# Which queue carries the divisions and the sum rows in a fused decay-attention and MLP kernel

## The chip, the cores and the metric

The kernel runs on one core of a Trainium2 chip. Its metric is the time of one execution in device microseconds, lower is better; a version's figure is the median of its runs. The profile is of one execution, whose own time is given beside its span. The engines are TensorE (PE, with its weight loads listed apart), VectorE (DVE), ScalarE (ACT), GpSimd (POOL) and SyncE (SP). SP computes nothing and issues transfers; GpSimd computes and issues a few too. A transfer is queued by the engine that issues it, and an engine works through its own instructions in order: one that waits holds all behind it.

## The reference

Causal attention with a decay, for 8 batches of 8 heads, 576 positions and head width 64, and then a two-layer MLP with a squared ReLU on the 4608 rows that come out. All inputs and outputs are float32.

```python
scores = scale * np.matmul(q, k.transpose(0, 1, 3, 2))
log_f = np.log(np.clip(f, 0.0001, 1.0))
cum = np.cumsum(log_f, axis=-1)
decay = cum[:, :, :, None] - cum[:, :, None, :]
causal = np.triu(np.ones((S, S), dtype=bool), k=1)
scores = np.where(causal, -1000000000.0, scores + decay)
scores = scores - np.max(scores, axis=-1, keepdims=True)
attn = np.exp(scores)
attn = attn / (np.sum(attn, axis=-1, keepdims=True) + 1e-09)
attn_out = np.matmul(attn, v)
x = attn_out.transpose(0, 2, 1, 3).reshape(B * S, H * D)
h = np.maximum(x @ w_in, 0.0)
out = h * h @ w_out          # x: 4608 x 512, w_in: 512 x 2048, w_out: 2048 x 512
```

## The kernel before

The 64 heads (8 batches of 8) go one after the other through six *units* each, a unit being a block of 64 to 128 keys against up to 448 queries. One *slot* of the main loop is one unit of the current head: its scores (L423 for the first ten heads, L425 and L428 later), the mask (L433), the exponential on ACT (L440, tiles `ph` and `pl` in turn), and, two slots later, the multiplication by v (L487), so that head h reads its `v` from slot 6h + 2 on. In the same slots the row maxima of the next head are taken: a product of rounded q and k on PE (L376), reduced on DVE (L384), and for the first ten heads turned on PE (L407) and copied by ACT (L411) into the row that the scores use.

For the first ten heads q and k exist twice: in a *rounded* tile (`rk`, two buffers, loaded by `load_rounded` on GpSimd's queue, L292) for the maxima, and in a *whole* tile (`rl`, two buffers, loaded by `load_whole` on SP, L299) for the scores. Each tile has, below its 64 rows of k, two rows with the high and the low part of the head's cumulative sum. They come from `decay`, which computes all heads' sums at the start in the tile `qkraw`; `store_cum` (L176) writes them to device memory as `cum_dr`, and `load_cum` fetches a head's two rows from there (L286). Only head 0 takes them straight from `qkraw`, in two transfers of one row (L284).

After two heads, `finish` divides by their sums in four parts: part 0 spreads the two rows of sums `den` over 128 partitions (`cmp`, L512); part 1 adds the epsilon and inverts on DVE (L514, L515) and stores the result (`rdr`, L517); part 2 reads it back, broadcast (`den`, L520); part 3 multiplies on GpSimd (L523). Part 0 stands in slot 6(h + 1) + 1 of the odd head h, parts 1, 2 and 3 three slots apart for the first eight heads. Heads 6 and 7 are divided on chip instead (`finish_here`).

The MLP's weights are 32 blocks of 512 KB, w_in and w_out in turn (`w0`, `w1`, ...). `weight_ops` loads them on SP (L195), up to four ahead, and rebuilds and splits each in steps on ACT (L206, L211) and DVE (L230, L235, L238, L242, L217), spread over the slots. The MLP (L591, L606 to L609, L621) begins after head 7 and then shares the slots with the later heads' attention.

On PE, ACT, DVE and GpSimd the order is that in which the program is written: `in_order` at its end ties each instruction to the one before it. On SP that holds only for what stands ahead of the main loop (`start`); the other transfers on SP are put in order by the framework's scheduler, by when it reckons that each can go. So moving a transfer from SP to GpSimd's queue fixes its place there, and may shift others on SP.

Of the kernel before, what the change touches and what calls it, by code (L numbers as in the profile page):

```python
# [34 lines left out]
def decay_attention_relu2_kernel(  # L35
# [18 lines left out]
    nc = tc.nc  # L54

    NH, D, _, S = qk.shape
    P = 2 * D
    H = 8
# [25 lines left out]
    def bank(use):  # L84
# [11 lines left out]
        out=mz[:, MW - P:], in_=mz[:, MW - P:], pattern=[[-1, P]],  # L96
# [6 lines left out]
        out=eye, in_=eye, pattern=[[-1, P]],  # L103
# [21 lines left out]
    def planes(pool, dtype, name):  # L125
        return Planes(pool.tile([P, S + SK], dtype, name=name))

    rounded = [planes(cpool, F32R, f"rk_{i}") for i in range(2)]
    whole = [planes(wk, F32, "rl") for _ in range(2)]
# [3 lines left out]
    def f32(x):  # L133
        return x if x.dtype == F32 else x.bitcast(F32)
# [16 lines left out]
    cum_dr = dr.tile([NH, 2, S], F32, name="cum_dr", bufs=1)  # L151
    fr = wk.tile([P, NCC, S], F32, name="xt0", bufs=1)
    cum, cums = [], []
# [4 lines left out]
    def decay():  # L158
        ft, zt, ct = (fr[:NH, i, :] for i in range(3))
        nc.vector.memset(zt, 0.0)  # L160
        constant_rows(nc.vector, rounded[0])
        nc.vector.tensor_scalar(ft, ft, 1e-4, 1.0, ALU.max, ALU.min)
        nc.scalar.activation(out=ft, in_=ft, func=AF.Ln)
        warm_exp = wk.tile([P, 8], F32, name="tcol")
        nc.vector.memset(warm_exp[:, :1], 0.0)
        nc.scalar.activation(out=warm_exp[:, :1], in_=warm_exp[:, :1], func=AF.Exp)
        nc.vector.tensor_tensor_scan(ct, zt, ft, 0.0, ALU.add, ALU.add)
        chl = wk.tile([P, 2, S], F32R, name="qkraw", bufs=1)
        ch, cl = chl[:, 0, :], chl[:, 1, :]
        nc.vector.tensor_copy(out=ch[:NH], in_=ct)  # L170
        nc.vector.tensor_tensor(out=cl[:NH], in0=ct, in1=ch[:NH].bitcast(F32), op=ALU.subtract)
        cum.extend(x.bitcast(F32) for x in (ch, cl))
        cums.append(chl[:NH].bitcast(F32))

    def store_cum():
        nc.sync.dma_start(out=cum_dr, in_=cums[0])  # L176
# [82 lines left out]
    def convert(n):  # L259

        for _ in range(n):
            next(weights, None)
# [7 lines left out]
    NU = len(UNITS)  # L270
# [6 lines left out]
        nc.sync.dma_start(out=raw, in_=qk[h])  # L277
        raws[h] = raw

    def load_cum(h, k, r=D):  # L280

        if h == 0:
            for i, c in enumerate(cum):
                nc.sync.dma_start(out=f32(k[r + i:r + i + 1, :S]), in_=c[h:h + 1])  # L284
        else:
            nc.sync.dma_start(out=f32(k[r:r + 2, :S]), in_=cum_dr[h])  # L286

    def load_rounded(h, rows=True):

        x = rounded[h % 2]  # L290
        state[h] = dict(r2=x.q, kl0=x.k, p={})
        nc.gpsimd.dma_start(out=x.raw[:D], in_=qk[h])  # L292
        if cum and rows:
            load_cum(h, x.k)

    def load_whole(h):

        x = state[h]["whole"] = whole[h % 2]
        nc.sync.dma_start(out=x.raw[:D], in_=qk[h])  # L299
        if cum:  # L300
            load_cum(h, x.k, D + 1)

    def load_v(h):
        if h < NH:
            vr = state[h]["vr"] = wk.tile([P, NJ, D + 2], F32, name="v", bufs=3)
            nc.sync.dma_start(out=vr[:, :, :D], in_=v[h])
            if h < NPLAIN:
                nc.gpsimd.memset(vr[:, :, D:], 1.0)

    def prep(h, part):  # L310

        if h >= NPLAIN + 4:
            prep_split(h, part)
            return
        if part == 0:
            x = planes(wk, F32R, "rl")
            (r2, kl0), (r1, l2) = ((x.q, x.k) for x in (rounded[h % 2], x))
            st = state[h] = dict(r2=r2, kl0=rounded[h % 2].k, r1=r1, l2=l2, p={}, raw=raws.pop(h))
            load_cum(h, kl0)
            nc.gpsimd.memset(f32(x.k[:, S:]), 0.0)  # L320
            nc.vector.tensor_copy(out=r2[:D], in_=st["raw"][:, 0, :])
            nc.vector.tensor_copy(out=kl0[:D, :S], in_=st["raw"][:, 1, :])
            nc.sync.dma_start(out=f32(l2[D:, :S]), in_=f32(kl0[:D, :S]))
        st = state[h]
        q, k = (st["raw"][:, i, :] for i in range(2))
        if part == 1:
            nc.sync.dma_start(out=f32(st["r1"][:D]), in_=f32(st["r2"][:D]))
        if part == 2:
            nc.vector.tensor_tensor(
                out=st["l2"][:D, :S], in0=k, in1=st["kl0"][:D, :S].bitcast(F32), op=ALU.subtract,  # L330
            )
        if part == 3:
            nc.vector.tensor_tensor(out=st["r1"][D:], in0=q, in1=st["r2"][:D].bitcast(F32), op=ALU.subtract)
# [170 lines left out]
    def finish(h, part):  # L504

        st = state[h]
        den = st["den"]
        if part == 0:
            st["cmp"] = wk.tile([P, 10], F32, name="cmp")[:, :S // D]

            for i in range(2):
                nc.sync.dma_start(out=st["cmp"][i * D:(i + 1) * D], in_=den[i * D:i * D + 1, :])  # L512
        if part == 1:
            nc.vector.tensor_scalar_add(st["cmp"], st["cmp"], EPS)  # L514
            nc.vector.reciprocal(out=st["cmp"], in_=st["cmp"])  # L515
            st["rdr"] = dr.tile([2, S], F32, name="rdr")
            nc.sync.dma_start(out=st["rdr"].rearrange("h (p c) -> (h p) c", p=D), in_=st["cmp"])  # L517
        if part == 2:
            for i in range(2):
                nc.sync.dma_start(out=den[i * D:(i + 1) * D], in_=st["rdr"][i:i + 1].broadcast_to([D, S]))  # L520
        if part == 3:
            x = xts[h // H][:, (h % H) // 2, :]
            nc.gpsimd.tensor_tensor(out=x, in0=x, in1=den, op=ALU.mult)  # L523
            del state[h], state[h - 1]
# [155 lines left out]
    VLOAD, VSPLIT = 2, 4  # L680
# [16 lines left out]
    for h in range(1, NH, 2):  # L697
        if h == H - 1:
            for part, n in enumerate((h * NU + 4, (h + 1) * NU + 2, (h + 1) * NU + 3)):
                fins.setdefault(n, []).append((finish_here, h - (part == 0), part))  # L700
            continue
        for part in range(4):
            fins.setdefault(fin(h, part), []).append((finish, h, part))
# [33 lines left out]
    def at(n, half, do, *args):  # L737
        events.setdefault((n, half), []).append(lambda: do(*args))
# [6 lines left out]
    for h in range(NH):  # L745
        split = h >= NWHOLE
        if split:
            at((h - 2) * NU + LOAD, 0, load, h)
            for part in range(4):
                at((h - 1) * NU + SPLIT[part], 1, prep, h, part)  # L750
        else:
            if h > 1:
                at((h - 3) * NU + 3, 0, load_rounded, h)
                at((h - 2) * NU + 5, 1, load_whole, h)
        at((h - 1) * NU + VLOAD, 1, load_v, h)
        at((h - 1) * NU + VSPLIT, 1, split_v, h)
        for i, x in enumerate(MAXIMA[split]):
            at((h - 1) * NU + int(x), int(2 * x) % 2, max_unit, h, i)
        if not split:
            at((h - 1) * NU + (4 if h else 3), 0, turn_maxima, h)  # L760
# [11 lines left out]
    spin(36)  # L772
    load_f()
    load_rounded(0)
    load_whole(0)
    constants()
    convert(1)
    decay()
    load_cum(0, rounded[0].k)
    load_cum(0, whole[0].k, D + 1)  # L780
    store_cum()
    convert(1)
    load_rounded(1, False)
    load_whole(1)
    load_cum(1, rounded[1].k)
    start = {i.name for i in tc.nc.cur_bb.bb.instructions}
    for n in range(-2 * NU, last_slot + 1):
        live = 0 <= n < len(slots)
        split_last()
        if live:  # L790
            h, u = slots[n]
# [65 lines left out]
```

## Time and profile before

| | us |
|---|---|
| runs of the kernel before | 1212.32, 1205.28, 1214.65 (median 1212.32) |
| the profiled execution's own time | 1208.21 |
| its span | 1206.5 |
| PE busy | 1178.1 (98%) |
| DVE busy | 784.9 (65%) |
| ACT busy | 684.6 (57%) |
| POOL busy | 316.9 (26%) |

The page's row of forty slices of 30.2 us, each digit the share of a slice in tenths that the 16 DMA engines were busy, shows that transfers crowd into the first five:

```profile
DMA  7785722221212121111110212112121112000000
```

A busy PE is an average over two regimes: the first slices, where attention alone runs and every engine waits now and then for another, and the rest, where the MLP's products fill PE. A name such as `rk<-cum_dr` is written tile, arrow, source; SPq is SP's queue. In the timelines a row has its start, its length, the engine, the line, the operation, the tiles and the count, and in brackets how long the engine had been idle and what ended that.

### The profile page before, as it was taken

What the parts mean: (1) busy time and instruction counts of PE and PEld (TensorE: products, weight loads), DVE (VectorE), ACT (ScalarE), POOL (GpSimd) and SP (SyncE); (2) the same over time, 40 slices, a digit from 0 to 9 for tenths busy, and PEclk for the clock granted to TensorE, in tenths of its full rate; (3) what the DMA queues carried; (4) which work ended last, traced back from release to release, by engine and by line L of the source; (5) the groups of instructions that cost most, each with busy time, mean ns of one, the idle gap of its engine ahead of it and who ended that gap; (6) DMA issues with size and microseconds to landing.
All of it is one profiled execution on the core that took longest, in us unless ns stands there. A gap on an engine that the chain in (4) does not pass through costs nothing. (4 is left out here: it accounts for less than half of the span.)

```text
span 1206.5 us, 23195 instructions
## 1 busy us (share of the span) xinstructions
PE 1178.1 (98%) x7786; PEld 1040.9 (86%) x7786; DVE 784.9 (65%) x2096; ACT 684.6 (57%) x1716; POOL 316.9 (26%) x511
## 2 busy tenths in 40 slices
PE   8999999999999999999999999999999999999998
PEld 4667877789998989899999899988999899999997
DVE  5889987766766676666656667666666766543332
ACT  3765555546666566656565566666566666533232
POOL 2110000213434343422222343334333434200000
PEclk9999999999999999999999999999999999999999
DMA  7785722221212121111110212112121112000000
GB/s 204 194 209 165 196 54 46 74 67 35 51 42 60 42 55 43 50 42 35 36 50 17 59 38 54 38 43 59 42 54 36 47 42 59 12 28 18 1 19 18
DMA packets 109798, 73.33 MB, mean 61 GB/s; under 512 B 90720, under 2 KB 90720, under 8 KB 109680
## 3 DMA queue, kind: packets, MB, share of 16 engines
q1 hardware_dynamic: 108880, 68.90, 22.4%
q0 software_dynamic: 800, 2.95, 1.1%
q8 instruction: 62, 1.02, 0.4%
q14 instruction: 56, 0.46, 0.1%
HBM read 58.71 MB, written 9.87 MB: 57 GB/s over the span
## 5 line engine op out<-in xcount | busy, mean ns | idle before, releaser
L621 PE MATMUL bank<-w,gh 128*128 128x512 f32 x1152 | 413.5, 399 | 0.0
L591 PE MATMUL bank<-xh,w 128*128 128x256 f32 x2304 | 331.6, 286 | 5.3 <-ACT r L606 5.1
L591 PEld LDWEIGHTS bank<-xh,w 128*128 128x128 f32 x2304 | 300.1, 189 | 16.8 <-ACT r L606 9.3
L456 DVE TENSOR_TENSOR pl<-p,ph 128x320 fp32r<-128x320 f32 (+4 forms) x288 | 175.4, 610 | 200.6 <-ACT ph L455 195.1
L621 PEld LDWEIGHTS bank<-w,gh 128*128 128x128 f32 x1152 | 217.5, 189 | 37.9
L621 PE MATMUL bank<-w,gl 128*128 128x512 f32 x576 | 227.1, 394 | 0.2 <-DVE gl L609 0.2
L455 ACT CAST ph<-p 128x320 fp32r<-128x320 f32 (+4 forms) x288 | 119.4, 415 | 162.0 <-POOL p L442 119.2
L607 DVE TENSOR_TENSOR g<-r 128x256 f32<-128x256 f32 x288 | 124.3, 432 | 102.0 <-ACT r L606 101.7
L442 POOL TENSOR_SCALAR_AFFINE_SELECT p<-p 128x128 f32<-128x128 f32 (+1 forms) x240 | 85.9, 358 | 396.1 <-ACT p L440 328.2
L606 ACT ACTIVATE r<-bank 128x256 f32<-128x256 f32 x288 | 109.7, 381 | 137.1 <-PE bank L591 124.5
L591 PE MATMUL bank<-xl,w 128*128 128x256 f32 x1152 | 184.8, 283 | 0.0
L440 ACT ACTIVATE p<-bank 128x320 f32<-128x320 f32 (+4 forms) x288 | 111.2, 386 | 117.9 <-PE bank L428 105.9
L384 DVE CUSTOM_DVE_ANT_0 bank<-bank,mz 128x256 f32<-128x256 f32 (+4 forms) x320 | 133.6, 431 | 50.6 <-PE bank L376 50.2
L609 DVE TENSOR_TENSOR gl<-g,gh 128x256 fp32r<-128x256 f32 x288 | 139.1, 483 | 34.4 <-PE bank L621 1.0
L591 PEld LDWEIGHTS bank<-xl,w 128*128 128x128 f32 x1152 | 158.5, 191 | 0.2 <-DVE xl L577 0.2
L608 ACT ACTIVATE gh<-r 128x256 fp32r<-128x256 f32 x288 | 120.4, 418 | 9.2
L376 PE MATMUL bank<-rk 66*128 66x320 f32 (+4 forms) x384 | 109.1, 314 | 13.4 <-DVE tcol L384 8.4
L621 PEld LDWEIGHTS bank<-w,gl 128*128 128x128 f32 x576 | 109.2, 190 | 15.0 <-DVE gl L609 1.7
L428 PE MATMUL bank<-rl 128*128 128x320 f32 x324 | 95.1, 294 | 0.0
L425 PE MATMUL bank<-rk 67*128 67x320 f32 x324 | 93.4, 288 | 0.0
L376 PEld LDWEIGHTS bank<-rk 66*128 66x128 f32 (+1 forms) x384 | 67.1, 181 | 30.4 <-DVE tcol L384 12.8
L466 PE MATMUL bank<-pl,vh 128*65 128x320 f32 (+4 forms) x336 | 91.3, 272 | 0.0
(97 smaller groups left out, 1478.8 us busy)
## 6 DMA issues: line engine op xcount, KB each, us to landing
qkraw<-in_qk SPq DMA_DIRECT2D x54, 288.0 KB
v<-in_v SPq DMA_DIRECT2D x64, 160.0 KB
out<-osb SPq DMA_DIRECT2D x36, 256.0 KB
den<-rdr SPq DMA_DIRECT2D x62, 144.0 KB
w<-in_w_in SPq DMA_DIRECT2D x16, 512.0 KB
w<-in_w_out SPq DMA_DIRECT2D x16, 512.0 KB
rk<-tcol SPq DMA_DIRECT2D x216, 0.5 KB
rl<-in_qk SPq DMA_DIRECT2D x10, 288.0 KB
```

Of the source, the lines that this page charges most:

```text
L376: nc.tensor.matmul(ps[:m, :n], st["r2"][:D + 2, q0:q0 + m], st["kl0"][:D + 2, k0:k0 + n], start=True, stop=True,)
L384: nc.vector.tensor_tensor_reduce(out=ps[:m, :n], in0=ps[:m, :n], in1=mz[:m, mo:mo + n], op0=ALU.add, op1=ALU.min, scale=-1.0, scalar=init, ...
L428: nc.tensor.matmul(ps[:kn, :n], st["l2"][:, k0:k0 + kn], st["r1"][:, q0:q1], start=False, stop=not added,)
L440: nc.scalar.activation(out=p[:kn, :n], in_=ps[:kn, :n], func=AF.Exp, scale=SCALE)
L455: nc.scalar.copy(out=ph[:kn, :n], in_=p[:kn, :n])
L456: nc.vector.tensor_tensor(out=pl[:kn, :n], in0=p[:kn, :n], in1=ph[:kn, :n].bitcast(F32), op=ALU.subtract,)
L591: nc.tensor.matmul(ph[:, :T], w[:, s, cc], x[:, cc, :], start=(cc == 0 and k == 0), stop=(cc == NCC - 1 and k == 2),)
L606: nc.scalar.activation(out=r, in_=ph[:, :T], func=AF.Relu)
L607: nc.vector.tensor_tensor(out=g, in0=r, in1=r, op=ALU.mult)
L608: nc.scalar.activation(out=gh, in_=r, func=AF.Square)
L609: nc.vector.tensor_tensor(out=gl, in0=g, in1=gh.bitcast(F32), op=ALU.subtract)
L621: nc.tensor.matmul(po, g[:, ts], w[:, s], start=(fc == 0 and k == 0), stop=(fc == NF - 1 and k == 2),)
```

## The change

Four things are changed. Head 1's sum rows for its rounded tile are copied from `qkraw` as head 0's are, ahead of `store_cum`. The rounded tiles' sum rows of the later first ten heads go on GpSimd's queue, behind the load of the same tile. The transfers of `finish` go on GpSimd's queue while h is under 8, that is for heads 1, 3 and 5. And at the start `load_v(0)` stands ahead of the step of the weights that loads the first w_out block, while head 1's rows for its whole tile are fetched behind that.

```diff
-    def load_cum(h, k, r=D):
-
-        if h == 0:
+    def load_cum(h, k, r=D, stored=True, queue=nc.sync):
+
+        if stored:
+            queue.dma_start(out=f32(k[r:r + 2, :S]), in_=cum_dr[h])
+        else:
             for i, c in enumerate(cum):
-                nc.sync.dma_start(out=f32(k[r + i:r + i + 1, :S]), in_=c[h:h + 1])
-        else:
-            nc.sync.dma_start(out=f32(k[r:r + 2, :S]), in_=cum_dr[h])
+                queue.dma_start(out=f32(k[r + i:r + i + 1, :S]), in_=c[h:h + 1])
...
         if cum and rows:
-            load_cum(h, x.k)
-
-    def load_whole(h):
+            load_cum(h, x.k, queue=nc.gpsimd)
+
+    def load_whole(h, rows=True):
...
-        if cum:
+        if cum and rows:
             load_cum(h, x.k, D + 1)
...
         den = st["den"]
+        queue = nc.gpsimd if h < H else nc.sync
         if part == 0:
...
-                nc.sync.dma_start(out=st["cmp"][i * D:(i + 1) * D], in_=den[i * D:i * D + 1, :])
+                queue.dma_start(out=st["cmp"][i * D:(i + 1) * D], in_=den[i * D:i * D + 1, :])
...
-            nc.sync.dma_start(out=st["rdr"].rearrange("h (p c) -> (h p) c", p=D), in_=st["cmp"])
+            queue.dma_start(out=st["rdr"].rearrange("h (p c) -> (h p) c", p=D), in_=st["cmp"])
...
-                nc.sync.dma_start(out=den[i * D:(i + 1) * D], in_=st["rdr"][i:i + 1].broadcast_to([D, S]))
+                queue.dma_start(out=den[i * D:(i + 1) * D], in_=st["rdr"][i:i + 1].broadcast_to([D, S]))
...
-        at((h - 1) * NU + VLOAD, 1, load_v, h)
+        if h:
+            at((h - 1) * NU + VLOAD, 1, load_v, h)
...
-    load_cum(0, rounded[0].k)
-    load_cum(0, whole[0].k, D + 1)
+    load_cum(0, rounded[0].k, stored=False)
+    load_cum(0, whole[0].k, D + 1, stored=False)
+    load_rounded(1, False)
+    load_cum(1, rounded[1].k, stored=False)
     store_cum()
+    load_whole(1, False)
+    load_v(0)
     convert(1)
-    load_rounded(1, False)
-    load_whole(1)
-    load_cum(1, rounded[1].k)
+    load_cum(1, whole[1].k, D + 1)
```

On SP, at the start of the program, this stands before (rk_0 and rk_1 are the rounded tiles of the even and odd heads, rl_81 and rl_82 the whole ones, w1 the first w_out block, v_197 head 0's v):

```order
L284 DMA rk_0_79<-qkraw_156 1x16x36 x2
L284 DMA rl_81<-qkraw_156 1x16x36 x2
L176 DMA cum_dr_85<-qkraw_156 64x1152
L195 DMA w1_164<-in_w_out 128x1024
L299 DMA rl_82<-in_qk 64x1152
L286 DMA rl_82<-cum_dr_85 2x576
L286 DMA rk_1_80<-cum_dr_85 2x576
L306 DMA v_197<-in_v 128x5x64
L286 DMA rk_0_79<-cum_dr_85 2x576
L195 DMA w2_243<-in_w_in 128x1024
```

And now (v_168 is head 0's v):

```order
L286 DMA rk_0_79<-qkraw_156 1x16x36 x2
L286 DMA rl_81<-qkraw_156 1x16x36 x2
L286 DMA rk_1_80<-qkraw_156 1x16x36 x2
L176 DMA cum_dr_85<-qkraw_156 64x1152
L299 DMA rl_82<-in_qk 64x1152
L306 DMA v_168<-in_v 128x5x64
L195 DMA w1_171<-in_w_out 128x1024
L283 DMA rl_82<-cum_dr_85 2x576
L195 DMA w2_244<-in_w_in 128x1024
```

Head 1's rounded rows have gone ahead of the store, v ahead of the first w_out block, and nothing waits for `cum_dr` until after that block.

On SP, around the division of heads 0 and 1, before (v_457 is head 3's v, v_558 head 4's):

```order
L299 DMA rl_82<-in_qk 64x1152
L286 DMA rl_82<-cum_dr_85 2x576
L512 DMA cmp_434<-den_317 64x1x9 x2
L195 DMA w7_445<-in_w_out 128x1024
L306 DMA v_457<-in_v 128x5x64
L286 DMA rk_1_80<-cum_dr_85 2x576
L517 DMA rdr_480<-cmp_434 128x9
L299 DMA rl_81<-in_qk 64x1152
L286 DMA rl_81<-cum_dr_85 2x576
L195 DMA w8_520<-in_w_in 128x1024
L520 DMA den_317<-rdr_480 64x576 x2
L306 DMA v_558<-in_v 128x5x64
```

And now, from the same whole tile (head 3's) on, up to head 6's v (the second rl_82 is head 5's whole tile):

```order
L299 DMA rl_82<-in_qk 64x1152
L283 DMA rl_82<-cum_dr_85 2x576
L195 DMA w7_446<-in_w_out 128x1024
L306 DMA v_458<-in_v 128x5x64
L195 DMA w8_521<-in_w_in 128x1024
L306 DMA v_559<-in_v 128x5x64
L299 DMA rl_81<-in_qk 64x1152
L283 DMA rl_81<-cum_dr_85 2x576
L195 DMA w9_594<-in_w_out 128x1024
L306 DMA v_655<-in_v 128x5x64
L195 DMA w10_663<-in_w_in 128x1024
L195 DMA w11_740<-in_w_out 128x1024
```

The five transfers of the division are gone, and weight blocks and v loads have closed up. Behind w11 stand head 5's whole tile, its sum rows and then head 6's v.

On GpSimd, at the same division, before (rk_0 at the first row is head 4's tile):

```order
L292 DMA rk_0_79<-in_qk 64x1152
L308 MEMSET v_457 128x5x2
L292 DMA rk_1_80<-in_qk 64x1152
L308 MEMSET v_558 128x5x2
L292 DMA rk_0_79<-in_qk 64x1152
L523 TENSOR_TENSOR xt0_316<-xt0_316,den_317 128x576
```

And now:

```order
L292 DMA rk_0_79<-in_qk 64x1152
L283 DMA rk_0_79<-cum_dr_85 2x576
L513 DMA cmp_435<-den_318 64x1x9 x2
L308 MEMSET v_458 128x5x2
L292 DMA rk_1_80<-in_qk 64x1152
L283 DMA rk_1_80<-cum_dr_85 2x576
L518 DMA rdr_481<-cmp_435 128x9
L521 DMA den_318<-rdr_481 64x576 x2
L308 MEMSET v_559 128x5x2
L292 DMA rk_0_79<-in_qk 64x1152
L283 DMA rk_0_79<-cum_dr_85 2x576
L524 TENSOR_TENSOR xt0_317<-xt0_317,den_318 128x576
```

Each load of a rounded tile is followed by its sum rows, and the division's transfers stand between the loads of heads 4, 5 and 6. The orders on PE, ACT and DVE are the same before and after.

## The prediction

> **What bounds the kernel now.** I read first the busy time by stretches, to see where TensorE (PE) is not full. Behind the stretch and its length each row has PE, weight loads, VectorE (DVE), ScalarE (ACT) and GpSimd (POOL), as busy us with the count of instructions, then the granted clock, the DMA share and GB/s.
>
> ```profile
> 0.00:80.00 80.00, 70.93 (x377) 45.20 (x378) 58.22 (x178) 49.58 (x116) 15.10 (x45) 0.98 0.78 195
> 80.00:180.00 100.00, 96.93 (x629) 79.19 (x628) 89.12 (x225) 57.65 (x136) 5.76 (x16) 1.00 0.55 153
> 260.00:600.00 340.00, 338.29 (x2308) 308.93 (x2307) 229.22 (x622) 208.43 (x531) 121.66 (x183) 1.00 0.19 44
> ```
>
> From 260 us on PE is full, and the change keeps the order of its instructions, so nothing can be won there except by arriving earlier. The change acts in the first 80 us, where PE is idle 80 - 70.93 = 9.1 us. So I read next what PE waited for there (us in total, times, longest), and what SyncE's queue waited for (SP, which issues most transfers, in order):
>
> ```profile
> PE bank L376 <- DMA rk<-cum_dr: 2.6, 1, 2.6
> PE bank L487 <- DMA v<-in_v: 2.0, 1, 2.0
> PE bank L487 <- ACT w L211: 1.2, 1, 1.2
> ...
> SPq L520 <- DMA rdr<-cmp: 6.7, 3, 3.9
> ```
>
> Three PE waits carry 5.8 us, and SP stands still longest for transfers that the change takes off it. Last I read the clock, in the windows of 3.41 us around the two places where it drops (busy PE, clock, DMA share, GB/s):
>
> ```profile
> 17.88:21.29 3.41, 1.56 (x9) 1.00 1.07 350
> 21.29:24.70 3.41, 3.41 (x13) 0.50 0.69 217
> 239.74:243.15 3.41, 1.62 (x10) 1.00 0.40 90
> 243.15:246.57 3.42, 3.42 (x16) 0.50 0.02 0
> ```
>
> Both windows at half clock follow one in which PE was busy 46 to 47%. The first of these two holds the wait for head 1's rows.
>
> **The change, part by part.**
>
> *Head 1's rows copied on chip, v ahead of the first w_out block.* The first row is what POOL's queue took from issue to landing of a 288 KB load; the others are SP's, PE's and ACT's timelines.
>
> ```profile
> DMA to landing us min/median/max: 3.6/5.6/7.6
> ...
> 10.86 0.59 SPq L176 DMA_DIRECT2D cum_dr<-qkraw  x1
> 12.12 0.81 SPq L299 DMA_DIRECT2D rl<-in_qk  x1
> 14.84 0.64 SPq L306 DMA_DIRECT2D v<-in_v  x1
> ...
> 19.73 0.50 PE L376 MATMUL bank<-rk 66*128 66x256 f32 x2 [2.59 <-DMA rk<-cum_dr]
> 21.61 0.74 PE L487 MATMUL bank<-ph,v 128*65 128x320 f32 x1
> 25.34 0.49 PE L487 MATMUL bank<-ph,v 128*65 128x192 f32 x2
> ...
> 21.20 0.65 ACT L206 ACTIVATE wmag<-w 128x512 f32<-128x512 f32 x1
> ```
>
> The two copies cost SP 2 x 0.6 = 1.2 us and go out from 10.86 to 12.1. With even the shortest landing of a load 128 times as large, 3.6, they are there by 15.7, and PE gets to them at 19.73 - 2.59 = 17.1: the 2.6 us go. What is late next stands behind them.
>
> v(0) is issued at 10.86 + 1.2 + 0.59 + 0.81 = 13.5 instead of 14.84, and 512 KB no longer stand ahead of it, some 2.0 us at the 217 to 350 GB/s of these windows. What is ahead starts 1.2 later, so it lands 0.8 earlier than before, which was by 21.61. PE now wants it at 21.61 - 2.6 = 19.0: a wait of 0 to 1.8; I take 0.8, near the middle, as no row says how long it had been there.
>
> The first w_out block has 448 KB more ahead of it (1.7 us) and the 1.2, so it lands 2.9 later than a landing that lay between 11.5 + 3.6 and 21.20: at 18.0 to 24.1. ACT stands in order behind it, and its next exponential ends 0.65 + 0.33 us later. PE wants that at 25.34 - 1.8 = 23.5: a wait of 0 to 1.6; I take 0.4, since most of that span ends before 23.5.
>
> The half clock cost up to 3.41 / 2 = 1.7. With the wait shorter by 1.8 the window before it would be busy far above 47%. I count 1.2, since PE would have waited for others in part of it.
>
> Sum -2.6 + 0.8 + 0.4 - 1.2 = **-2.6**, between -4.3 (no new wait, all of the 1.7) and +0.8 (both waits full, the clock as before). Head 1's rows for its scores, now behind the w_out block, are read after head 0's units, to which the row at 25.34 still belongs: nothing.
>
> The Trainium skill (TensorE: Matmul & The Clock Gate, What's actually happening) has the clock halved after an idle window of some 3.4 us. The rows disagree: here a window with PE busy 46% was enough. By that rule the wait of 2.6 would have cost no clock and this sum would be -1.4.
>
> *SP without the divisions and the rounded tiles' rows.*
>
> ```profile
> 34.84 3.73 SPq L512 DMA_DIRECT2D cmp<-den  x2
> 39.30 0.58 SPq L306 DMA_DIRECT2D v<-in_v  x1
> 45.91 0.72 PE L487 MATMUL bank<-ph,v 128*65 128x320 f32 x2 [1.18 <-ACT w L211]
> ...
> 49.72 0.48 SPq L299 DMA_DIRECT2D rl<-in_qk  x1
> 62.84 0.59 SPq L306 DMA_DIRECT2D v<-in_v  x1
> 70.50 0.72 PE L487 MATMUL bank<-ph,v 128*65 128x320 f32 x2 [2.01 <-DMA v<-in_v]
> 71.35 0.37 DVE L384 CUSTOM_DVE_ANT_0 bank<-bank,mz 128x192 f32<-128x192 f32 x1 [1.42 <-PE bank L376]
> ```
>
> PE's multiplication at 45.91 reads v(3). The profile puts the wait down to a cast on ACT, which it doesn't read; v(3), issued at 39.30 behind SP's stand of 3.73 us, can be late, and in the new order it goes out at about 35. I count the 1.2 as gone (0 to 1.2, the first if it was ACT). v(6), issued at 62.84, now waits on SP only for head 5's whole tile, whose load went out at 49.72: the 2.0 go for PE, while DVE gets back 1.42 there; I take **-1.7**, between the two. Weight blocks go out earlier too; PE's waits name none, so that wins nothing.
>
> *The same transfers on POOL's queue*: the divisions of heads 1, 3 and 5, and the rows of heads 2 to 9.
>
> ```profile
> POOL rk L292 <- PE bank L433: 35.0, 6, 7.9
> ...
> 37.69 0.36 ACT L502 COPY den<-bank 1x256 f32<-1x256 f32 x1
> 40.14 0.16 DVE L514 TENSOR_SCALAR cmp<-cmp 128x9 f32<-128x9 f32 x1
> 42.62 0.43 DVE L384 CUSTOM_DVE_ANT_0 bank<-bank,mz 128x256 f32<-128x256 f32 x1 [1.06 <-PE bank L376]
> ...
> 53.34 0.36 ACT L502 COPY den<-bank 1x256 f32<-1x256 f32 x1
> 57.15 0.16 DVE L514 TENSOR_SCALAR cmp<-cmp 128x9 f32<-128x9 f32 x1
> 58.89 0.43 DVE L384 CUSTOM_DVE_ANT_0 bank<-bank,mz 128x256 f32<-128x256 f32 x1 [1.05 <-PE bank L376]
> ...
> 68.16 0.36 ACT L502 COPY den<-bank 1x256 f32<-1x256 f32 x1
> 74.83 0.17 DVE L514 TENSOR_SCALAR cmp<-cmp 128x9 f32<-128x9 f32 x1 [1.01 <-DMA cmp<-den]
> 75.91 0.42 DVE L384 CUSTOM_DVE_ANT_0 bank<-bank,mz 128x256 f32<-128x256 f32 x1
> ```
>
> POOL stood 35.0 us for PE ahead of those loads, so its time to issue is hidden. What counts is L, from issue to landing of `cmp<-den` there, for DVE stands in order at L514. From the end of `den` to L514 are 2.1, 3.5 and (less the wait) 5.3 us, and behind the first two DVE has gaps of 1.06 and 1.05. So the cost is max(0, L - 3.15) + max(0, L - 4.5) + max(0, L - 5.3) - 1.01, the last being the wait that it has at 74.83. With L of 3.6 that is -0.6, with 5.6 +2.8, with 7.6 +8.8. A transfer of 2 KB is nearest to the shortest load, but weight blocks that SP no longer holds back will run beside it, so I take 4.6: 1.45 + 0.1 - 1.01 = **+0.5**. Below -1.0 it can't go. POOL then stands at `den<-rdr` until `rdr` has landed, for head 3 by 57.5 + 7.6 = 65.1 at the latest. The load behind it lands 7.6 later at the worst, 72.7, and head 8, which it serves, starts on DVE at 75.91: hidden.
>
> **Sum.** -2.6 - 1.2 - 1.7 + 0.5 = -5.0. The profiled execution took 1208.21 (span 1206.5 and 1.7 around it), 4.1 below the median of 1212.32; the runs, 1205.28 to 1214.65, lie on both sides of it. I start in the middle, at 1210.3, and forecast **1205**.
>
> **Rivals.**
> 1. *Slower: divisions that land late on POOL's queue.* From L = 6.5 on, the cost, by then 3L - 13.96, eats the other -5.5. For it: the 7.6 in the row. Against: that load moves 128 times the bytes. At 7.6 it gives 8.8 - 5.5 = +3.3, 1214. The Trainium skill (SBUF — State Buffer, A bandwidth-pool intuition that's wrong (but worth ruling out)) says that GpSimd can't write its descriptors while certain DVE operations hold the port they share, which speaks against the move. Whether the spread from 3.6 to 7.6 comes of that, no row tells.
> 2. *Hidden by DVE.* From 80 to 180 us DVE is busy 89.12 of 100. If it carries that stretch, only what DVE itself gets back counts, the 1.42 just before it, and PE's lead is spent: 1209. Against: DVE waits for PE at the start of each head (42.62, 58.89).
> 3. *More.* All of the -4.3, the waits of 1.2 and 2.0, DVE's 1.0, and the window at 243 us at full clock, another 1.7: -10.2, 1200. For it: that window falls where 3.41 us windows happen to lie. Against: the idle time ahead of it is none that the change removes.
>
> **How the numbers follow.** The forecast has 0.53 (1202 to 1208), rival 2 has 0.2, rival 3 0.14, rival 1 0.13. 1198 to 1213 leaves out most of rival 1 and the end of rival 3. A measurement of this kernel tells about 1%, 12 us, from no change. Faster by more than that takes more than rival 3's sum, or luck of the runs: 0.1. Slower by more lies beyond rival 1: 0.03. Within: 0.87.
>
> **What the profile will show.** Head 1's first L376 without a wait for its rows; clock 1.00 from 17 to 28 us; no wait of PE for v after 25 us; SP nowhere standing for a division before 80 us; DVE at L514 waiting under 1.5 us for head 1 and not at all for head 5; from 260 us on the same as now, 5 us earlier. I am wrong if PE waits at 20 us for v or ACT as long as it had for the rows, or if L is above 6.

## The result, and the profile after

| | kernel before | changed kernel |
|---|---|---|
| median of the runs, us | 1212.03 (1205.28 to 1214.65, 4 runs) | 1223.67 (1219.38 to 1225.55, 4 runs) |
| profiled execution, us | 1208.21 | 1219.38 |
| its span, us | 1206.5 | 1217.7 |
| its mean granted clock | 0.997 | 0.992 |

The ratio is 1.0100, with a 95% interval of 1.0051 to 1.0149: the changed kernel is slower by about 1%. The forecast was 1205 with a range of 1198 to 1213, so both the sign and the range were wrong.

First the stretches that were shown of before, of the changed kernel (stretch, its length, then busy us and count of PE, weight loads, DVE, ACT and POOL, the granted clock, DMA share, GB/s):

```profile
0.00:80.00 80.00, 67.40 (x334) 42.27 (x335) 49.96 (x159) 44.13 (x102) 26.78 (x64) 0.91 0.84 207
80.00:180.00 100.00, 95.00 (x608) 76.35 (x607) 86.55 (x222) 58.84 (x140) 7.66 (x19) 1.00 0.51 140
260.00:600.00 340.00, 336.67 (x2295) 307.24 (x2293) 228.30 (x617) 208.76 (x532) 121.35 (x183) 1.00 0.19 46
```

In the first 80 us PE ran 334 matmuls where it ran 377 before, and DVE was busy 49.96 us where it was 58.22: less was done in the same time. A mark that can be found in both traces is the first score product of L428, which comes with the heads behind the tenth. Its row (count, duration ns min/median/max, first and last start in us, shapes) is for before

```profile
L428 PE MATMUL bank<-rl x324: 220/296/372, 112.3 to 1047.3; 128*128 128x320 f32 x54, 128*128 128x192 f32 x54, 128*128 128x448 f32 x54
```

and for the changed kernel

```profile
L428 PE MATMUL bank<-rl x324: 220/296/372, 122.0 to 1058.1; 128*128 128x320 f32 x54, 128*128 128x192 f32 x54, 128*128 128x448 f32 x54
```

So 9.7 of the 11.2 us by which the span grew are there by 122 us, and the last of these products is late by 10.8: what follows the first hundred microseconds only carries the loss on. The waits of the changed kernel in its first 80 us, of DVE and then of SP's queue (who, for whom; us in total, times, longest), say what took the place of the old ones:

```profile
DVE cmp L515 <- DMA cmp<-den: 12.3, 2, 10.1
```

```profile
SPq L299 <- PE bank L487: 34.9, 6, 11.7
```

SP waits for no division any more, as the change means it to; what it waits for most is PE, which has to set a whole tile free (34.9 us). In return DVE stands at the epsilon of the division (L515 now, L514 before). The timeline of the changed kernel, here of DVE, ACT, POOL and PE in turn, shows the longest of those stands, in the division of heads 2 and 3:

```profile
42.96 0.17 DVE L515 TENSOR_SCALAR cmp<-cmp 128x9 f32<-128x9 f32 x1 [2.22 <-DMA cmp<-den]
67.19 0.17 DVE L515 TENSOR_SCALAR cmp<-cmp 128x9 f32<-128x9 f32 x1 [10.10 <-DMA cmp<-den]
84.63 0.17 DVE L515 TENSOR_SCALAR cmp<-cmp 128x9 f32<-128x9 f32 x1 [3.19 <-issue]
...
53.93 0.36 ACT L502 COPY den<-bank 1x256 f32<-1x256 f32 x1
...
55.44 2.92 POOL L524 TENSOR_TENSOR xt<-xt,den 128x576 f32<-128x576 f32 x1 [5.06 <-DMA den<-rdr]
58.31 1.11 POOL L513 DMA_DIRECT2D cmp<-den  x2
...
68.35 0.64 PE L376 MATMUL bank<-rk 66*128 66x320 f32 x1 [7.30 <-DVE tcol L384]
```

Read it from ACT on. The sums were ready at 53.93 + 0.36 = 54.3. GpSimd's next instruction was the multiplication of the division before, whose broadcast reciprocals had not landed; it began at 55.44 and took 2.92 us, so the sums' copies were issued only at 58.31. The second of them left GpSimd's issue slot at about 59.4, and DVE could start at 67.19. DVE had stood since 57.1, with the row maxima behind it, and PE stood 7.30 us for them. The three stands sum to 2.22 + 10.10 + 3.19 = 15.5 us; before there was one, of 1.01. (The profile puts the third down to `issue`; it is counted here because by the trace that copy landed at 84.54, right ahead of L515.)

The clock is the other part. Windows of the changed kernel, with the columns as above:

```profile
20.87:24.28 3.41, 2.24 (x15) 1.35 (x14) 2.09 (x6) 2.81 (x8) 0.25 (x2) 1.00 1.05 417
24.28:27.70 3.42, 3.42 (x9) 1.87 (x9) 1.95 (x7) 2.15 (x5) 0.00 (x0) 0.50 1.24 281
27.70:31.11 3.41, 3.41 (x14) 2.50 (x12) 1.56 (x7) 2.04 (x6) 0.00 (x0) 0.50 1.12 243
...
61.83:65.24 3.41, 0.00 (x0) 0.00 (x0) 0.00 (x0) 0.00 (x0) 0.00 (x0) 1.00 1.17 199
65.24:68.66 3.42, 0.31 (x1) 0.31 (x2) 1.43 (x6) 0.70 (x2) 0.48 (x1) 0.50 1.15 226
68.66:72.07 3.41, 3.41 (x13) 2.44 (x13) 3.41 (x12) 1.98 (x6) 0.13 (x2) 0.50 0.37 71
```

From 61.83 to 65.24 no engine of the core computes anything, while the DMA share is 1.17. Counted by the same PE instruction in both traces, the changed kernel was 2.8 us ahead at head 1's first row maximum (16.95 against 19.73), had lost that by 31 us in the two windows at half clock, stood within 1 us of level until 57, and was behind by 8.1 at 68.35 and by 9.9 at 72.

### The profile page after: what moved, and what is told of

It reads as the page before. It is cut to its first block, busy times and chain, and to the rows that moved or that the text cites. A ratio compares the mean times of both kernels' runs of the same rounds, so it can differ in the third digit from the quotient of the medians.

```text
span 1217.7 us, 23195 instructions
## 1 busy us (share of the span) xinstructions
PE 1182.4 (97%) x7786; PEld 1043.3 (86%) x7786; DVE 781.5 (64%) x2096; ACT 684.8 (56%) x1716; POOL 332.1 (27%) x534
## 5 line engine op out<-in xcount | busy, mean ns | idle before, releaser
L610 DVE TENSOR_TENSOR gl<-g,gh 128x256 fp32r<-128x256 f32 x288 | 130.3, 452 | 35.5 <-ACT p L440 1.9
L376 PE MATMUL bank<-rk 66*128 66x320 f32 (+4 forms) x384 | 111.4, 319 | 21.4 <-DVE tcol L384 17.0
L376 PEld LDWEIGHTS bank<-rk 66*128 66x128 f32 (+1 forms) x384 | 68.2, 183 | 39.7 <-DVE tcol L384 22.2
L428 PE MATMUL bank<-rl 128*128 128x320 f32 x324 | 95.2, 294 | 0.0
```

Of the source, the lines that this page charges most:

```text
L376: nc.tensor.matmul(ps[:m, :n], st["r2"][:D + 2, q0:q0 + m], st["kl0"][:D + 2, k0:k0 + n], start=True, stop=True,)
L428: nc.tensor.matmul(ps[:kn, :n], st["l2"][:, k0:k0 + kn], st["r1"][:, q0:q1], start=False, stop=not added,)
L610: nc.vector.tensor_tensor(out=gl, in0=g, in1=gh.bitcast(F32), op=ALU.subtract)
```

## The experiments

Two theories were set against each other first. A says that the loss is DVE's stand at L515, made by the divisions' new queue; its rivals put it down to another part of the change. Within A, one reason (A1) is that GpSimd's order issues the copies late, behind the multiplication of the division before; the other (A2) is that the copies are long under way because SP, which no longer stands at a division, fills the DMA engines with weight blocks. All ratios are to the kernel before, run beside it on the same chip. The times expected were reckoned from 1212 us for the kernel before; beside these runs it took 1206 to 1209, so it is the ratio that tells. The column of blocks has the weight blocks that SP issued between 30 and 65 us.

| run | time, us | before, us | ratio, 95% interval | DVE's stands for heads 1, 3, 5, us | mean clock | blocks |
|---|---|---|---|---|---|---|
| changed kernel | 1223.67 | 1212.03 | 1.0100, 1.0051 to 1.0149 | 2.2, 10.1, 3.2 | 0.992 | 9 |
| div_on_sp | 1207.11 | 1209.36 | 0.9974, 0.9947 to 1.0002 | none | 1.000 | 6 |
| div_only | 1224.70 | 1209.36 | 1.0128, 1.0065 to 1.0191 | 2.5, 4.2, 6.6 | 0.987 | 7 |
| start_only | 1207.38 | 1209.36 | 0.9966, 0.9933 to 0.9999 | 0, 0, 0.3 | 0.996 | 6 |
| rows_only | 1209.00 | 1209.36 | 0.9990, 0.9961 to 1.0020 | 0, 0, 2.6 | 0.997 | 7 |
| mult_later | 1221.78 | 1207.98 | 1.0101, 1.0055 to 1.0147 | 2.0, 3.1, 3.5 | 0.978 | 9 |
| part0_sp | 1213.62 | 1207.98 | 1.0041, 1.0018 to 1.0064 | 0, 3.3, 3.7 | 0.992 | 9 |
| part0_act | 1225.10 | 1207.98 | 1.0138, 1.0098 to 1.0177 | 4.6, 0, 0.4 | 0.990 | 6 |
| depth2 | 1229.10 | 1207.98 | 1.0164, 1.0110 to 1.0218 | 4.5, 4.1, 3.6 | 0.977 | 10 |
| no_w | 1204.23 | 1209.26 | 0.9970, 0.9950 to 0.9990 | none | 0.997 | 0 |
| no_w_sp | 1206.15 | 1209.26 | 0.9973, 0.9959 to 0.9987 | none | 0.998 | 0 |
| best | 1212.06 | 1209.26 | 1.0011, 0.9986 to 1.0037 | 0, 2.5, 0 | 0.997 | 7 |
| gate | 1214.23 | 1206.01 | 1.0084, 1.0051 to 1.0116 | 0, 5.9, 2.2 | 0.996 | 6 |

The kernel before had stands of 0, 0 and 1.0 us, a clock of 0.997 and 7 blocks. The clock is that of the profiled execution, as the stands and the blocks are; the ratio with its interval comes from all the runs, and isn't the quotient of the medians to the last digit.

**The changed kernel with the divisions back on SP (div_on_sp).**

```diff
-        queue = nc.gpsimd if h < H else nc.sync
+        queue = nc.sync
```

> The changed kernel with the divisions' transfers back on SP; all else as changed. Theory A (the loss is VectorE standing at the inversion, 2.2, 10.1 and 3.2 us at the three divisions, for sums that land late by GpSimd's queue): those waits go, about 10 us come back, so 1212 to 1215, and the first product of the split scores (PE L428) starts at 111 to 114 us instead of 122.0. Theory B (the loss is the half clock at 24 to 31 us, and weight blocks that go out in bursts): 1220 to 1224, L428 first at 120 to 123.

The loss is gone, and more than that: 1207.11, below the range of A. In its first 80 us SP stands at the divisions again,

```profile
SPq L521 <- DMA rdr<-cmp: 9.9, 3, 3.8
SPq L513 <- ACT den L502: 3.5, 2, 2.0
```

DVE has no stand for them, and the mark of L428, and PE's busy time in the first 80 us, are better than before (112.3 and 70.93 there):

```profile
L428 PE MATMUL bank<-rl x324: 220/296/371, 107.2 to 1041.4; 128*128 128x320 f32 x54, 128*128 128x192 f32 x54, 128*128 128x448 f32 x54
```

```profile
0.00:80.00 80.00, 73.69 (x410) 47.78 (x411) 60.85 (x188) 52.66 (x124) 20.52 (x55) 1.00 0.84 212
```

L428 starts earlier than A expected, too. A single line of the change thus carries all of the loss. The half clock of theory B went with the stands (the clock is 1.000 here), so this run alone doesn't part A from B; the next two do.

**The kernel before with only the divisions on GpSimd's queue (div_only).**

```diff
+        queue = nc.gpsimd if h < H else nc.sync
...
-                nc.sync.dma_start(out=st["cmp"][i * D:(i + 1) * D], in_=den[i * D:i * D + 1, :])
+                queue.dma_start(out=st["cmp"][i * D:(i + 1) * D], in_=den[i * D:i * D + 1, :])
...
-            nc.sync.dma_start(out=st["rdr"].rearrange("h (p c) -> (h p) c", p=D), in_=st["cmp"])
+            queue.dma_start(out=st["rdr"].rearrange("h (p c) -> (h p) c", p=D), in_=st["cmp"])
...
-                nc.sync.dma_start(out=den[i * D:(i + 1) * D], in_=st["rdr"][i:i + 1].broadcast_to([D, S]))
+                queue.dma_start(out=den[i * D:(i + 1) * D], in_=st["rdr"][i:i + 1].broadcast_to([D, S]))
```

> The kernel before with only the divisions' transfers of heads 1, 3 and 5 on GpSimd's queue. Theory A: VectorE stands 8 us or more in all at the inversions before 90 us, and the time is 1218 to 1224. Theory B: no more than 1 us above before, 1211 to 1213. If the late landing needs the rounded rows on GpSimd's queue too, something between.

The same loss comes without any other part of the change, and DVE's stands with it:

```profile
DVE cmp L515 <- DMA cmp<-den: 13.2, 3, 6.6
```

So the move is enough by itself, as it is needed, and theory A stands. There are no more blocks between 30 and 65 us than before, 7.

**The start alone (start_only), and the rounded tiles' rows alone (rows_only).** The first is the kernel before with head 1's rows copied on chip and v ahead of the first w_out block; the second has only this:

```diff
-            load_cum(h, x.k)
+            load_cum(h, x.k, queue=nc.gpsimd)
```

> The kernel before with only the start changed: head 1's rounded rows copied on chip and v ahead of the first w_out block. Theory A: no loss, PE gets to head 1's first L376 at 17 instead of 19.7 us and keeps 0 to 3 us of it: 1209 to 1212. Theory B: ScalarE waits 2 to 3 us for the first w_out block, a window at half clock follows, and the time is 1213 to 1217.

> The kernel before with only the rounded tiles' sum rows on GpSimd's queue. Both theories: SP is freed of two stands of 3.0 and 3.5 us for PE, nothing waits longer, 1210 to 1213. If GpSimd's queue itself were what costs, 1215 or more.

The start alone wins 0.3%, with an interval that just excludes no change. Head 1's first L376 starts at 16.70 instead of 19.73, and PE keeps a lead of 2 to 4 us until 370 us, which the profiled execution then loses in a window at half clock. This is the start that the changed kernel has, without the loss, so theory B fails. The rows alone change nothing that can be measured. Neither is where the loss is.

**The multiplication later in GpSimd's order (mult_later).** If A1 were the whole of it, taking the multiplication from ahead of the next copies would do.

```diff
-    DIVIDE = (2, 5, 8, 11), (2, 4, 6, 7)
+    DIVIDE = (2, 5, 8, 15), (2, 4, 6, 7)
```

> The changed kernel with the multiplications of heads 1, 3 and 5 four slots later, so that on GpSimd they stand behind the next division's first transfer instead of ahead of it. Theory A1 (the sums are late because their transfer stands behind the multiplication, which waits for the division before): VectorE's wait at head 3's division falls from 10.1 to 2 us or less, 1210 to 1214. Theory A2 (they are late because the transfer takes 8 us beside SP's weight blocks): only the 4.0 us from the end of den to the issue go, the wait stays at 5 to 7 us, 1216 to 1221.

For head 3 the copies now went out at 52.60, 0.3 us behind the sums' end at 52.31, and still landed 6.45 us later. Head 3's stand fell to 3.1 us, between the 2 of A1 and the 5 to 7 of A2, and the three to 8.6, but the time did not follow. One longer stand came, of DVE in the division on chip of heads 6 and 7:

```profile
DVE cmp L545 <- PE bank L542: 3.9, 1, 3.9
```

And the profiled execution ran at half clock for 31 us from 82.5 on. So A1 has a share in the long stand of head 3, but removing it isn't enough: what is left is under way too long. With so much half clock, though, the time doesn't test the stands alone.

**Only the sums' copies back on SP (part0_sp), or on ACT's queue with the rest on SP (part0_act).** These ask whether it is GpSimd's queue as such that is slow.

```diff
-                queue.dma_start(out=st["cmp"][i * D:(i + 1) * D], in_=den[i * D:i * D + 1, :])
+                nc.sync.dma_start(out=st["cmp"][i * D:(i + 1) * D], in_=den[i * D:i * D + 1, :])
```

```diff
-        queue = nc.gpsimd if h < H else nc.sync
+        queue = nc.sync
...
-                queue.dma_start(out=st["cmp"][i * D:(i + 1) * D], in_=den[i * D:i * D + 1, :])
+                nc.scalar.dma_start(out=st["cmp"][i * D:(i + 1) * D], in_=den[i * D:i * D + 1, :])
```

> The changed kernel with only the first of a division's transfers (cmp from den) back on SP; rdr and the broadcast stay on GpSimd's queue. If the first transfer's landing is all of the loss (A1 or A2): VectorE waits under 1 us in all at the inversions, 1206 to 1211 as with the whole division on SP. If the later ones cost too, by holding GpSimd in front of the rounded loads and so PE: 1213 to 1219 with PE waiting for a rounded tile.

> The changed kernel with the first transfer of all divisions issued by ScalarE, which writes den itself and so waits for nothing there, and the rest of the divisions on SP. If a queue other than SP's is slow beside the weight blocks, whichever engine it belongs to: VectorE waits 5 us or more at head 3, 1214 to 1222. If it is GpSimd's queue that is slow: landing within 3 us, no wait, SP not held, 1204 to 1209.

Rows of part0_sp, of SP and of DVE:

```profile
51.17 0.49 SPq L513 DMA_DIRECT2D cmp<-den  x1
...
57.27 0.17 DVE L515 TENSOR_SCALAR cmp<-cmp 128x9 f32<-128x9 f32 x1 [3.34 <-DMA cmp<-den]
```

and of part0_act, of ACT and of DVE:

```profile
35.46 0.48 ACTq L513 DMA_DIRECT2D cmp<-den  x1
...
42.21 0.17 DVE L515 TENSOR_SCALAR cmp<-cmp 128x9 f32<-128x9 f32 x1 [4.63 <-DMA cmp<-den]
```

and, for head 5 in the kernel before, of SP and of DVE:

```profile
66.11 2.92 SPq L512 DMA_DIRECT2D cmp<-den  x2
...
74.83 0.17 DVE L514 TENSOR_SCALAR cmp<-cmp 128x9 f32<-128x9 f32 x1 [1.01 <-DMA cmp<-den]
```

On SP's queue DVE went 57.27 - 51.66 = 5.6 us behind the end of the issue, on ACT's 42.21 - 35.94 = 6.3 us, and in the kernel before, on SP's, 74.83 - 69.03 = 5.8. So the long way isn't a property of GpSimd's queue, and it isn't new with the change either. Neither expectation for part0_sp held: DVE still stood 7.0 us, and in the main loop PE waited for no rounded tile. With the copies out of GpSimd's order it has less than half of the loss. part0_act missed too: its stand came at head 1, not at head 3. It has small stands and a large loss: its edit puts the copies of all 31 such divisions in ACT's order, and PE fell further behind, from 9.0 us at 390 us to 16.8 at 1054. Its time says nothing on the question; its row does.

**Weight blocks only two ahead (depth2).**

```diff
-    DEPTH = 4
+    DEPTH = 2
```

> The changed kernel with weight blocks loaded two ahead instead of four, so that fewer stand in SP's queue beside a division. A2: the first transfers take 5 us or less from issue to landing, VectorE's waits at the inversions fall below 8 us in all, 1212 to 1218. A1: no change in them, 1220 to 1225. It can lose elsewhere if ScalarE then waits for weight blocks.

This missed: the copies took longer, not shorter (median from issue to landing 6.4 us, against 5.0 in the changed kernel), and the time was the worst of all. Between 30 and 65 us SP issued 10 weight blocks, against 9 in the changed kernel and 7 before. The bound of two limits how many are ahead of their use, not when they go; it spread no block and so didn't test A2.

**No weight loads (no_w), and the same with the divisions on SP (no_w_sp).** This takes the suspected load away.

```diff
-                raw = staged[i] = wk.tile([P, 2 * DM], I32, name=f"w{i}", bufs=1)
+                if i > 1:
+                    staged[i] = staged[i - 2]
+                    return
+                raw = staged[i] = wk.tile([P, 2 * DM], I32, name=f"w{NW - 2 + i}", bufs=1)
```

> The changed kernel without the loads of 30 of the 32 weight blocks (all blocks are rebuilt from the first two, so the MLP's part of the output is left wrong); every engine's work stays, 15 MB of transfers go. A2 (the division's first transfer is slow only because weight blocks that SP no longer holds back fill the DMA engines): it takes 2 to 3.5 us on GpSimd's queue from issue to landing, VectorE waits under 2 us in all at the inversions, and the time is 1198 to 1208. If GpSimd's queue itself is slow: it still takes 5 us or more, VectorE waits 5 us or more, 1212 to 1220.

> The same without the weight loads, and with the divisions back on SP: what the division's queue is worth when nothing competes. A2: within 3 us of the kernel without weight loads that has them on GpSimd's queue, 1198 to 1206. If GpSimd's queue is slow in itself: 8 us or more faster than that one.

The row of the transfers (issuing queue, count, size, median us from issue to landing) is, in the changed kernel and then in no_w:

```profile
cmp<-den POOLq DMA_DIRECT2D x6, 2.2 KB, 5.0
```

```profile
cmp<-den POOLq DMA_DIRECT2D x6, 2.2 KB, 1.8
```

Between 58 and 67 us, the stretch of the long stand, the changed kernel and no_w have

```profile
58.00:67.00 9.00, 3.04 (x14) 1.93 (x14) 0.00 (x0) 1.56 (x4) 2.48 (x6) 0.90 1.13 227
```

```profile
58.00:67.00 9.00, 8.55 (x53) 5.76 (x52) 8.72 (x26) 7.12 (x17) 4.30 (x7) 1.00 0.53 131
```

With the divisions still on GpSimd's queue, and with the multiplication still ahead of the next copies, the copies land in 1.8 us (1.7 to 3.1), just under what A2 expected, DVE has no stand, and the loss is gone: 0.997. For head 3 that multiplication ended there at 48.0, 1.3 us ahead of the sums (49.3), since the reciprocals too landed sooner. Without that traffic the queue costs nothing that can be measured: no_w and no_w_sp have the same ratio to 0.0003. So the weight traffic is needed for the loss, for the way of the copies and, through the late reciprocals, for the late issue. That is the first half of A2. The second, that SP's stands held back the blocks that are too much, isn't shown by taking away all blocks, and their number doesn't show it: div_only has the loss with as many as before.

What the copies wait for can be read from the landings in the traces. In the changed kernel, around head 3's division, they were

| transfer | queue | issued, us | landed, us |
|---|---|---|---|
| whole tile | SP | 57.17 | 63.84 |
| weight block | SP | 58.20 | 66.88 |
| first copy of the sums | GpSimd | 58.31 | 66.62 |
| second copy | GpSimd | 58.89 | 67.10 |
| rounded tile | GpSimd | 59.44 | 67.64 |

Transfers landed nearly in the order of their issue, on whatever queue, so a copy of 2.2 KB took as long as the large loads issued just ahead of it. It is the same where the copies are on SP: in the kernel before, a whole tile issued at 64.79 landed at 74.32 and head 5's copy of 68.55 at 74.74; in part0_sp a rounded tile of 47.51, on GpSimd's queue, landed at 56.85 and head 3's copy of 51.17 at 57.18. What counts is thus what is under way when a copy is issued, not how many blocks go out in all.

**SP made to stand again (gate).** The transfers that count stay on GpSimd's queue; SP gets small copies that nobody reads, with the divisions' waits.

```diff
+    gate = wk.tile([P, S // D], F32, name="gate", bufs=1)
...
+            if h < H:
+                for i in range(2):
+                    nc.sync.dma_start(out=gate[i * D:(i + 1) * D], in_=den[i * D:i * D + 1, :])
...
+        if part == 2 and h < H:
+            nc.sync.dma_start(out=gate, in_=st["rdr"].rearrange("h (p c) -> (h p) c", p=D))
```

> The changed kernel, with small copies on SyncE's queue that wait for the first eight heads' divisions as the transfers themselves did before (two behind the sums' copy, one behind the reciprocals), and whose data nobody uses; the transfers that count stay on GpSimd's queue. Theory A2 (sums land late because SyncE, which no longer stands at a division, fills the DMA engines with weight blocks): SyncE stands again, so the sums land sooner, in 2 to 4 us from issue rather than 4 to 8, VectorE's three waits at the inversions sum to under 8 us rather than 15.5, and the time is 1207 to 1216. Rival (GpSimd's in-order queue alone: its transfers stand behind the multiplication of the division before): nothing of that changes, the waits sum to 13 to 17 and the time stays at 1218 to 1226.

The stands sum to 8.1 us, about half of 15.5 and just above what A2 expected. The time, 1214.23, lies in A2's range only because the kernel before was faster beside it: the ratio, 1.0084, can't be told from the changed kernel's 1.0100. The median way of the copies was 5.7 us, not the 2 to 4 of A2. The rows of SP around the divisions of heads 1 and 3, and of GpSimd at head 3, show why:

```profile
32.20 4.26 SPq L518 DMA_DIRECT2D gate<-den  x2
...
47.49 0.50 SPq L518 DMA_DIRECT2D gate<-den  x1
48.10 0.57 SPq L306 DMA_DIRECT2D v<-in_v  x1
48.72 0.63 SPq L195 DMA_DIRECT2D w<-in_w_in  x1
49.44 0.47 SPq L299 DMA_DIRECT2D rl<-in_qk  x1
...
50.60 0.48 SPq L518 DMA_DIRECT2D gate<-den  x1
...
52.59 1.12 POOL L515 DMA_DIRECT2D cmp<-den  x2
```

For head 1 SP stood 4.26 us at its two copies and sent nothing between them; GpSimd's last copy, issued at 36.23, landed 1.9 us later, and DVE did not stand. For head 3 SP's scheduled order has loads of v, of a weight block and of a whole tile between its two copies, so SP did not stand; GpSimd's copies, issued late, at 52.59, landed at 59.29 and 59.94, behind that whole tile (58.34). Even SP's own copy of 50.60 landed only at 58.51, so an earlier issue would have won little. Where SP stood, the copies were protected; where it didn't, they weren't. That is the second half of A2, as far as one division shows it.

**The divisions on SP and the first w_out block ahead of v again (best).**

```diff
-        queue = nc.gpsimd if h < H else nc.sync
+        queue = nc.sync
...
+    convert(1)
     load_v(0)
-    convert(1)
```

> The changed kernel with the divisions back on SP and the first w_out block ahead of v again; head 1's rows on chip and the rounded rows on GpSimd's queue stay. If ScalarE's wait for that block (2.7 us in the changed kernel) cost anything at the end: it goes, and the time is 1 to 2 us below the kernel with only the divisions on SP, 1203 to 1206. If not, or if v is then late by as much, the same as that one, 1205 to 1209.

It missed: 1212.06, no better than before, with a PE wait of 1.3 us for v and a window at half clock. That speaks for v ahead of the block, but the interval reaches into that of div_on_sp, so it isn't shown. The best versions measured that still load all weights are div_on_sp and start_only, 0.26% and 0.34% under the kernel before; the first interval ends at 1.0002, the second at 0.9999, so they are barely told from no change and not from each other.

## Why the prediction was wrong

**The step that failed is the term of +0.5 for the divisions.** Its formula, max(0, L - 3.15) + max(0, L - 4.5) + max(0, L - 5.3) - 1.01, can stand; the L in it can't. It stood for issue to landing, taken as 4.6, with the issue right behind the sums. By the landings in the trace it was 4.0, 8.2 and 5.9 us for the last copy of heads 1, 3 and 5, and its issue began 0.3, 4.6 and 0.5 us behind the sums' end. With the sums' end to landing, 4.3, 12.8 and 6.5, the formula gives 1.15 + 8.3 + 1.2 - 1.01 = 9.6 instead of 0.5. That this is so near the 9.7 at L428 is partly luck: head 1's stand had cost PE nothing by 57 us, 1.9 us of the delay came in the window at half clock behind head 3's stand, and of the -5.5 of the other terms nothing was left. Two things were missed. The multiplication, which waits for the broadcast, stands at the end of the order shown for GpSimd, ahead of the next copies, and the prediction asked only how late the load behind it would be, not the copies. And L was put between the landings of the loads, near the shortest because the copy is small, where a copy lands behind the loads that are under way. The prediction's own rows had a case of it: at head 5 the sums end at 68.52 and DVE, after waiting for the copy, goes at 74.83, 6.3 us later.

**"Weight blocks go out earlier too; PE's waits name none, so that wins nothing"** priced only the gain. The DMA share between 30 and 65 us was 0.76 before and 0.91 in the changed kernel, with 9 weight blocks issued in place of 7; but div_on_sp has a share of 0.88, and its copies were in time, so these averages don't decide. What was overlooked is the order: before, SP sent nothing between the two copies of a division, for 2.9 to 3.7 us, and the last of them landed 1.8, 3.2 and 6.2 us after its issue. That stand was a protection of the very transfers that were moved, as gate's head 1 shows.

**Rival 1 is what happened**, by its mechanism, to which the prediction gave a chance of 0.13 and a price that stopped at an L of 7.6 and so at 1214. The rule that the prediction set beside it, the Trainium skill's in SBUF — State Buffer (A bandwidth-pool intuition that's wrong (but worth ruling out)), that GpSimd can't write descriptors while certain DVE operations hold their shared port, isn't the reason here: DVE did nothing from 57.1 to 67.19 us, while head 3's copies were under way, and in no_w it was busy 8.72 of 9 us and the copies of that stretch took 1.9 and 1.7.

**The start** was right in its main term: the wait of 2.6 went, and PE reached head 1's rows 2.8 us sooner. Of the new waits, that for v was none (0.8 was counted) and that for ACT behind the first w_out block was larger than the 0.4 counted, as these rows of ACT and PE in the changed kernel show:

```profile
21.43 0.66 ACT L206 ACTIVATE wmag<-w 128x512 f32<-128x512 f32 x1 [2.73 <-DMA w<-in_w_out]
...
22.36 0.54 PE L487 MATMUL bank<-ph,v 128*65 128x192 f32 x2 [1.12 <-ACT ph L440]
```

The 1.2 for the half clock had the wrong sign in the changed kernel: a window with PE busy 2.24 of 3.41, 66%, was followed by two at half clock, which took the whole lead by 31 us. In div_on_sp, which starts in the same way, the clock stayed at 1.00, and PE was 2.7 us ahead at 31 us, which is about the -2.6 that was summed. So this term came out either way with the same start, and a saving by it can't be counted on; why, is open.

**SP without the divisions** was right in what it removed, PE's waits for v at 45.91 and 70.50, and wrong in that they would be worth anything: with DVE standing 10 us PE has no use for v. What the prediction summed without the divisions, -5.5, is about what div_on_sp shows at L428, 107.2 against 112.3, but there SP still carries the divisions and PE has no wait for v either, so that likeness doesn't bear this term out; and its runs kept some 2 to 3 us of it.

**The signs named in advance** told it apart: L above 6 at the longest stand, and DVE's stands over the bounds given. The half clock from 24 to 31 us, where 1.00 was named, was a second one.

**Open.** How the 10.1 us of head 3 divide into late issue and long way depends on the order in which they are taken away: with the issue at 54.3 and the same way, 5.4 us of the stand would be left; with the late issue and a way of 1.8, 3.6. Nor do these runs say how much of the 1% is DVE's stands and how much the half clock that follows them. That SP's stands protect the copies rests on the landings and on one division of gate; no run held the traffic ahead of the copies alone fixed.

## What to carry to other kernels

A queue that stands still can also be a gate: before a small, urgent transfer is moved off it, ask what bulk transfers stood behind it there and will now be under way when it is issued. Price such a move by the time from the data's readiness to landing, with everything that stands ahead on the new engine, its computing included, and with the traffic as it will be after the change. And where an engine works in order, look at what stands behind the instruction that consumes the transfer, since its wait holds all of that. (In mult_later, moving it back shortened head 3's stand but not the time.)

## What was unexpected of the hardware

A copy of 2.2 KB on GpSimd's queue took from issue to landing 1.7 to 3.1 us without weight traffic and 1.8 to 8.3 with it, and about as long on the queues of SP and ACT (5.6 and 6.3 from the end of the issue to DVE's start). It landed in its turn behind the loads issued ahead of it on any queue. One pair in the changed kernel shows both ends, in these rows of GpSimd and SP:

```profile
77.38 0.59 POOL L513 DMA_DIRECT2D cmp<-den  x1
78.63 0.53 POOL L513 DMA_DIRECT2D cmp<-den  x1 [0.65 <-ACT den L502]
...
77.99 0.63 SPq L195 DMA_DIRECT2D w<-in_w_in  x1
78.66 0.43 SPq L195 DMA_DIRECT2D w<-in_w_out  x1
79.14 0.43 SPq L195 DMA_DIRECT2D w<-in_w_in  x1
```

The first copy landed 1.8 us after its issue, at 79.17; the second, issued 1.25 us later, behind the block of 77.99, after 5.9 us.

The half clock can last. In div_only it held for five windows, some 17 us, in four of which the profile has PE busy from end to end:

```profile
81.66:85.08 3.42, 0.00 (x0) 0.00 (x0) 0.38 (x3) 0.00 (x0) 0.00 (x0) 1.00 1.20 177
85.08:88.50 3.42, 2.21 (x7) 1.58 (x7) 3.21 (x12) 2.04 (x5) 0.57 (x1) 0.50 0.27 94
...
98.70:102.15 3.45, 3.45 (x11) 2.28 (x11) 2.17 (x6) 1.32 (x4) 0.00 (x0) 0.50 0.12 39
102.15:105.50 3.35, 3.35 (x24) 2.41 (x23) 2.23 (x12) 1.73 (x5) 0.00 (x0) 1.00 0.55 154
```

The Trainium skill (TensorE: Matmul & The Clock Gate, What's actually happening) has the clock back after one busy window of some 3.4 us. These rows agree on the fall, behind a window with PE at 0, and disagree on the return, though PE's ends are modelled and small gaps may hide in a busy window. A stand of an engine that feeds PE can therefore cost PE more than its own length, as mult_later and depth2, with the lowest clocks, suggest; no run here held the clock fixed to show it.
